# Attention over memory slots with a spatial gate: one load over all partitions each for k, v and phi, row reductions by halving, and a new written order

## The chip, the cores and the metric

The kernel runs on one core of a Trainium2 chip. The metric is the device time of one execution in microseconds (us). The engines are named as the profile names them: PE (TensorE, matmuls), PEld (its weight loads), DVE (VectorE), ACT (ScalarE), POOL (GpSimd) and SP (SyncE), whose queue SPq issues every transfer of this kernel.

## What is computed

The inputs are q, k, v of 8 batches x 8 heads x 576 rows x 64, and phi of 8 x 8 x 576 x 32. Cut to what matters:

```python
a = softmax(phi, over the 576 rows)                 # the maximum and the sum run over rows
k_m, v_m = a^T k, a^T v                             # 32 x 64 for each head
attn = softmax(q k_m^T / 8, over the 32 slots)
x = attn v_m, heads side by side                    # 8 x 576 x 512
h = relu(x w_in);  u, v = the halves of h           # 512 columns each
v_n = (v - mean) / sqrt(var + 1e-6)                 # over columns
v_s = w_spatial v_n + b_spatial                     # over the 576 rows
out = (u * v_s) w_out
```

The weights w_in (512 x 1024), w_spatial (576 x 576) and w_out (512 x 512) are the same for all batches. w_in and w_out arrive as 64-bit numbers, which the kernel turns into 32-bit ones by shifts, masks and multiplications ("decode").

## The kernel before

The work is cut into small generator functions, one step to each `yield`, named by a letter: P `memory_weights` (load of phi, its softmax), K `memories` (loads of k and v, k_m and v_m), Q `queries`, S `scores`, M `products` (v_m times w_in, so that x w_in becomes attn times that), V `gate`, U `units`, G `spatial`, O `project`. For the weights: D `load_win`, L and E decode of the two column halves of w_in, X load and decode of w_out, W and T w_spatial and its transposes, B the bias.

The order on every engine is written out by hand. START is the order of the prologue, of the whole of batch 0 and of what batch 1 needs meanwhile. PLAN is played once for each further batch; a prime marks the next batch, two primes the one after. All engines work off their instructions in this order, SP its transfers too. The set ON_VECTOR says which steps go to DVE; those not in it go to POOL, ACT or PE.

Products that need more than one pass of precision are split in a high and a low part, and the low part (`ml`, `wtl`, `ws`, `al`, `vl`, `gl`) is a difference. On DVE it is one subtraction. Elsewhere PE subtracts the high part in PSUM by a matmul with a negative identity (`minus`) and ACT copies the rest.

Names in the rows: `raw` is w_in as it arrives, `power` and `win_sb` are its decode, `raw_out` is w_out; `phi_sb` and `kv_sb` hold phi, k and v of one batch; `mx` is the maximum over the 9 row groups of a partition, `mt`, `cm`, `cmb` and `mb` finish it over partitions; `es` is the sum of the exponentials; `kvm` is the product of phi with k and v (72 matmuls a batch, then 8 with `ones` for the sum); `sc` are the scores, `sm` the scores turned, `aT`, `ah`, `al` the attention; `mp` is products' PSUM, `mh` and `ml` its parts; `pu`, `pv`, `ps`, `po` are the PSUM tiles of units, gate, spatial and project. `mp0` and `mp1` below are the two column halves of mp. There are four single-bank PSUM buffers (`bank`), which sc, mp, mt, mb, kvm, tk, tv, pv and po take in turn, and two double ones for wt, pu and ps.

A transfer of phi, k or v of a batch is two: heads of even number to partitions 0 to 63, heads of odd number to partitions 64 to 127. The queries of batch 0 come in a layout of their own: whole rows of 64 numbers, read once for either half of the columns, in 12 transfers; those of the other batches come in 4 transfers, in pieces of 32 numbers.

Of the kernel before, what the change touches and what calls it, by code (L numbers as in the profile page):

```python
# [51 lines left out]
    E0.add E1.add L0.add L0.mul ml001 wtl0 X0.add X1.add X1.mul X2.wol X3.mul ml110 ml111 ml100  # L52
    ml101
# [4 lines left out]
def memory_attention_spatial_gate(  # L58
# [12 lines left out]

# [349 lines left out]
    def queries(b, _):  # L421
        qT = None
        if b == 0:

            tiles = [
                one.tile([P, n, NX * D + 32], F32, tag=tag, name="q_all")
                for n, tag in ((4, "q_sb"), (2, "mh"), (2, "ml"))
            ]
            h = 0
            for x in tiles:  # L430
                n = x.shape[1]
                for c in range(2):
                    for g in range(2):
                        rows = slice(64 * c + 32 * g, 64 * c + 32 * g + 32)
# [4 lines left out]
                    yield  # L439
                h += n  # L440
            parts = [
                x[:, 2 * n : 2 * n + 2, 32:].rearrange("p h (i d) -> p h i d", d=D)[:, :, :, 0:32]
                for x in tiles
                for n in range(x.shape[1] // 2)
            ]
        else:
            q_sb = one.tile([P, H, NX, 32], F32, name="q_sb")
            for c in range(2):
                for g in range(2):
                    rows = slice(64 * c + 32 * g, 64 * c + 32 * g + 32)  # L450
                    nc.sync.dma_start(
                        q_sb[rows].rearrange("p h i d -> p (h i) d"),
                        q[b, :, :, 32 * g : 32 * g + 32].rearrange(
# [337 lines left out]
```

## Time and profile before

| | us |
|---|---|
| median of 3 runs | 441.12 (441.07 to 441.49) |
| the profiled execution | 442.75 |
| its span, first to last instruction | 440.9 |
| PE busy | 403.1 (91%) |
| DVE busy | 302.3 (69%) |
| ACT busy | 222.9 (51%) |
| POOL busy | 70.3 (16%) |

The span is that of the instructions; the execution's time has 1.8 us more around it. PE is the engine with most work, but its idle time is not spread over the span: the busy shares in 40 slices show it idle in the first five to six slices of 11 us and full from there on.

### The profile page before, as it was taken

How to read it: one execution, taken by the hardware profiler on the slowest of the kernel's cores; microseconds unless marked ns; L12 is line 12 of the kernel's file. 1: busy time of each engine (PE TensorE's matmuls, PEld its weight loads, DVE VectorE, ACT ScalarE, POOL GpSimd, SP SyncE). 2: the span in 40 equal slices, each digit the busy share in tenths (PEclk: the TensorE clock that was granted, in tenths of full speed). 3: DMA queues.
4: the chain of work that ended last, by engine and by line, in shares of the span. 5: the costliest groups of instructions: out<-in, count | busy, mean ns of one | idle time of the engine just before them, and what ended most of it. 6: DMA issues, size and time to landing. Idle time of an engine off the chain costs nothing.

```text
span 440.9 us, 9251 instructions
## 1 busy us (share of the span) xinstructions
PE 403.1 (91%) x3815; PEld 336.2 (76%) x3815; DVE 302.3 (69%) x501; ACT 222.9 (51%) x427; POOL 70.3 (16%) x147
## 2 busy tenths in 40 slices
PE   1425699999999999999999999999999999999996
PEld 1313178788879888898889887988798887988984
DVE  0973998998599538994699439955897457824420
ACT  3552367764583429532764248343843367336412
POOL 2033214430210004000400022001400021003000
PEclk9999999999999999999999999999999999999999
DMA  8999999922999129912992159903990300010003
GB/s 252 361 210 219 210 188 185 232 22 76 177 167 111 48 77 196 165 15 97 178 170 31 73 133 169 125 24 114 175 163 16 104 3 1 1 71 26 1 3 118
DMA packets 86863, 51.88 MB, mean 118 GB/s; under 512 B 66786, under 2 KB 70882, under 8 KB 86820
## 3 DMA queue, kind: packets, MB, share of 16 engines
q1 hardware_dynamic: 86820, 51.28, 58.5%
q8 instruction: 30, 0.49, 0.5%
q14 instruction: 13, 0.11, 0.1%
HBM read 41.83 MB, written 9.44 MB: 116 GB/s over the span
## 4 chain that ended last, share of the span: by engine, by line
PE 83%; DMA 11%; DVE 2%; ACT 2%; SPq 1%; issue 1%; POOL 0%; DVEq 0%; ACTq 0%; POOLq 0%
PE ps L658 27%; PE po L698 22%; PE pv L571 12%; PE pu L620 11%; PE kvm L365 4%; DMA q_all<-in_q_dram 4%; DMA kv_sb<-in_v_dram 3%; PE mp L541 3%; DMA raw<-in_moe_w_in_dram 2%; PE sc L480 2%; DMA phi_sb<-in_phi_dram 1%; DVE mx L322 1%; SPq L352 0%; DVE vl L598 0%; ACT vr L593 0%
## 5 line engine op out<-in xcount | busy, mean ns | idle before, releaser
L658 PE MATMUL ps<-wth,vh 128*128 128x288 f32 x256 | 57.8, 307 | 0.1
L658 PE MATMUL ps<-wtl,vh 128*128 128x288 f32 x256 | 54.9, 296 | 0.0
L658 PE MATMUL ps<-wth,vl 128*128 128x288 f32 x256 | 54.6, 295 | 0.0
L583 POOL TENSOR_SCALAR rs<-mv 128x1 f32<-128x1 f32 (+1 forms) x40 | 8.8, 221 | 269.4 <-DVE mv L580 245.2
L698 PE MATMUL po<-woh,gh 128*128 128x512 f32 x128 | 49.9, 390 | 0.0
L698 PE MATMUL po<-woh,gl 128*128 128x512 f32 x128 | 49.9, 390 | 0.0
L698 PE MATMUL po<-wol,gh 128*128 128x512 f32 x128 | 49.8, 389 | 0.0
L704 ACT COPY o<-po 128x512 f32<-128x512 f32 x36 | 21.1, 589 | 54.7 <-PE po L698 53.9
L658 PEld LDWEIGHTS ps<-wth,vh 128*128 128x128 f32 x256 | 40.6, 189 | 10.0 <-issue 5.0
L578 DVE BATCH_NORM_STATS2 st<-vr 128x6 f32<-128x512 f32 (+1 forms) x40 | 27.3, 681 | 27.5 <-ACT vr L575 27.5
L680 ACT CAST gh<-g 128x512 fp32r<-128x512 f32 x32 | 19.1, 620 | 50.9 <-DVE g L669 50.9
L658 PEld LDWEIGHTS ps<-wtl,vh 128*128 128x128 f32 x256 | 41.3, 189 | 0.0
L658 PEld LDWEIGHTS ps<-wth,vl 128*128 128x128 f32 x256 | 41.3, 188 | 0.0
L629 ACT ACTIVATE u<-pu 128x576 f32<-128x576 f32 x32 | 20.2, 658 | 30.8 <-PE pu L620 30.4
L593 ACT ACTIVATE vr<-vr,sh,rs 128x512 f32<-128x512 f32 (+1 forms) x40 | 31.8, 816 | 4.8 <-POOL sh L588 4.8
L365 PE MATMUL kvm<-kv_sb,phi_sb 64*32 64x128 f32 x1152 | 24.9, 309 | 8.8 <-DMA kv_sb<-in_v_dram 8.8
L571 PE MATMUL pv<-mh,ah 128*128 128x512 f32 (+1 forms) x80 | 31.8, 397 | 0.0
L571 PE MATMUL pv<-mh,al 128*128 128x512 f32 (+1 forms) x80 | 31.6, 395 | 0.0
L571 PE MATMUL pv<-ml,ah 128*128 128x512 f32 (+1 forms) x80 | 31.6, 395 | 0.0
L365 PEld LDWEIGHTS kvm<-kv_sb,phi_sb 64*32 64x32 f32 x1152 | 19.5, 118 | 15.4 <-DMA kv_sb<-in_v_dram 9.3
L669 DVE TENSOR_TENSOR g<-u,ps 128x576 f32<-128x576 f32 x32 | 24.0, 752 | 10.1 <-PE ps L658 9.8
L682 DVE TENSOR_TENSOR grl<-g,grh 128x64 fp32r<-128x64 f32 x32 | 6.7, 212 | 34.8 <-ACT grh L680 34.8
(130 smaller groups left out, 896.3 us busy)
## 6 DMA issues: line engine op xcount, KB each, us to landing
kv_sb<-in_k_dram SPq DMA_DIRECT2D x16, 576.0 KB, 8.7
kv_sb<-in_v_dram SPq DMA_DIRECT2D x16, 576.0 KB, 8.3
out_dram<-o SPq DMA_DIRECT2D x32, 256.0 KB, 2.0
q_sb<-in_q_dram SPq DMA_DIRECT2D x28, 288.0 KB, 8.2
phi_sb<-in_phi_dram SPq DMA_DIRECT2D x16, 288.0 KB, 4.9
raw<-in_moe_w_in_dram SPq DMA_DIRECT2D x8, 512.0 KB, 7.5
raw_out<-in_moe_w_out_dram SPq DMA_DIRECT2D x4, 512.0 KB, 9.9
w_sb<-in_moe_w_spatial_dram SPq DMA_DIRECT2D x1, 1152.0 KB, 5.7
```

The source lines that it names most:

```text
L365: nc.tensor.matmul(kvm[r][32 * j : 32 * j + 32], phi_sb[halves[r], j, i, :], kv_sb[halves[r], j, :, i * D : (i + 1) * D], start=(i == 0), ...
L541: nc.tensor.matmul(mps[r][32 * j : 32 * j + 32, :], vT[D * r : D * r + D, 32 * j : 32 * j + 32], win_sb[D * r : D * r + D, j, cs], start=True,
L571: nc.tensor.matmul(pv, x[:, r, cs], m[:, r, DM:DFF], start=(n == 0), stop=(n == 5))
L578: nc.vector.bn_stats(st6, vr)
L593: nc.scalar.activation(vr, vr, AF.Identity, bias=sh, scale=rs)
L620: nc.tensor.matmul(pu[:, hf, 0:HALF], m[:, r, cs], a[:, r, hf * HALF : (hf + 1) * HALF], start=(n == 0), stop=(n == 5),)
L629: nc.scalar.activation(u[:, dt, :].rearrange("p (a s) -> p a s", a=2), pu[:, :, 0:HALF], AF.Relu)
L658: nc.tensor.matmul(ps[:, hf, 0:HALF], a, w[:, hf * HALF : (hf + 1) * HALF], start=(n == 0), stop=(n == len(ops) - 1),)
L669: nc.vector.tensor_tensor(g.rearrange("p (a s) -> p a s", a=2), u[:, dt, :].rearrange("p (a s) -> p a s", a=2), ps[:, :, 0:HALF], op=ALU.mult,
L680: nc.scalar.copy(hi, x)
L698: nc.tensor.matmul(po, a, w, start=(n == 0), stop=(n == 11))
L704: nc.scalar.copy(o, po)
```

## The change

Four edits, and a new order:

- phi, k and v of a batch come in one transfer each over 128 partitions (two heads side by side) in place of two over 64.
- q of batch 0 is loaded as in the other batches: 4 transfers in pieces of 32 numbers, 1.18 MB in all, in place of 12 transfers that move 2.36 MB.
- The maximum and the sum over a partition's 9 row groups are four elementwise instructions (`over_rows`: 4 groups against 4, 2 against 2, 1 against 1, and the ninth) in place of one reduction. `es` takes `mx`'s buffer. The sum of batch 1 runs on POOL, the others on DVE.
- START is written anew; PLAN differs only in that three P steps stand where one stood ahead (`P'*4`, `P''*4`). In ON_VECTOR the last multiplication of E's decode moves from POOL to DVE, and three low parts change places (`ml001` to `ml000`, `wtl0` to `wtl2`, `X2.wol` to `X3.wol`).

```diff
-        for r in range(2):
-            nc.sync.dma_start(
-                phi_sb[64 * r : 64 * r + 64].rearrange("p j i m -> p j (i m)"),
-                phi[b].rearrange("(j r) (p i) m -> r p j (i m)", r=2, i=NX)[r],
-            )
+        nc.sync.dma_start(
+            phi_sb.rearrange("p j i m -> p j (i m)"),
+            phi[b].rearrange("(j r) (p i) m -> (r p) j (i m)", r=2, i=NX),
+        )
...
-        nc.vector.tensor_reduce(mx, phi_sb.rearrange("p j i m -> p j m i"), axis=AX.X, op=ALU.max)
-        yield
+        yield from over_rows(nc.vector, mx, ALU.max)
...
-        es = state["es", b] = one.tile([P, NJ, MEM], F32, name="es")
-        nc.vector.tensor_reduce(es, phi_sb.rearrange("p j i m -> p j m i"), axis=AX.X, op=ALU.add)
-        yield
+        es = state["es", b] = one.tile([P, NJ, MEM], F32, tag="mx", name="es")
+        yield from over_rows(engine(f"es{b}"), es, ALU.add)
...
+    def over_rows(eng, to, op):
+        half = one.tile([P, NJ, 4, MEM], F32, name="half")
+        eng.tensor_tensor(half, phi_sb[:, :, 0:4], phi_sb[:, :, 4:8], op=op)
+        yield
+        eng.tensor_tensor(half[:, :, 0:2], half[:, :, 0:2], half[:, :, 2:4], op=op)
+        yield
+        eng.tensor_tensor(to, half[:, :, 0], half[:, :, 1], op=op)
+        yield
+        eng.tensor_tensor(to, to, phi_sb[:, :, 8], op=op)
+        yield
...
-            for r in range(2):
-                nc.sync.dma_start(
-                    kv_sb[64 * r : 64 * r + 64, :, n, :],
-                    x[b].rearrange("(j r) (p i) d -> r p j (i d)", r=2, i=NX)[r],
-                )
+            nc.sync.dma_start(
+                kv_sb[:, :, n, :], x[b].rearrange("(j r) (p i) d -> (r p) j (i d)", r=2, i=NX)
+            )
...
-        if b == 0:
...
-                        nc.sync.dma_start(
-                            x[rows, :, 32 - 32 * g : 32 - 32 * g + NX * D],
-                            q[b, h : h + n].rearrange("h (c x i) d -> c x h (i d)", c=2, i=NX)[c],
-                        )
...
+        q_sb = one.tile([P, H, NX, 32], F32, name="q_sb")
+        for c in range(2):
+            for g in range(2):
...
+                    q[b, :, :, 32 * g : 32 * g + 32].rearrange(
+                        "h (i c x) d -> c x (h i) d", c=2, x=32
+                    )[c],
...
-    P' K' U0 V1 V0 K' U0 V2 U0 K' U2 V0 V1 U1 V1 V0 V2 V1 V2 K' V0 V4 U1 V1 V3 Q' K' V0 P'' V1
+    P'*4 K' U0 V1 V0 K' U0 V2 U0 K' U2 V0 V1 U1 V1 V0 V2 V1 V2 K' V0 V4 U1 V1 V3 Q' K' V0 P'' V1
```

The first transfers of SP, before: w_spatial first, then phi, all of w_in, k, v, q of batch 0, and then phi, k and v of batch 1.

```order
1 L257 DMA w_sb<-in_moe_w_spatial_dram 128x4x576
2 L258 DMA w_rem<-in_moe_w_spatial_dram 64x576
3 L260 DMA b_sb<-in_moe_b_spatial_dram 1x576 x2
4 L316 DMA phi_sb<-in_phi_dram 64x4x288 x2
5 L175 DMA raw<-in_moe_w_in_dram 128x1024 x8
6 L352 DMA kv_sb<-in_k_dram 64x4x576 x2
7 L352 DMA kv_sb<-in_v_dram 64x4x576 x2
8 L435 DMA q_all<-in_q_dram 32x4x576 x4
9 L435 DMA q_all<-in_q_dram 32x2x576 x8
10 L316 DMA phi_sb<-in_phi_dram 64x4x288 x2
11 L352 DMA kv_sb<-in_k_dram 64x4x576 x2
12 L352 DMA kv_sb<-in_v_dram 64x4x576 x2
```

The same stretch of SP now:

```order
1 L174 DMA raw<-in_moe_w_in_dram 128x1024
2 L326 DMA phi_sb<-in_phi_dram 128x4x288
3 L256 DMA w_sb<-in_moe_w_spatial_dram 128x4x576
6 L174 DMA raw<-in_moe_w_in_dram 128x1024 x4
7 L359 DMA kv_sb<-in_k_dram 128x4x576
8 L174 DMA raw<-in_moe_w_in_dram 128x1024
9 L359 DMA kv_sb<-in_v_dram 128x4x576
10 L174 DMA raw<-in_moe_w_in_dram 128x1024 x2
11 L432 DMA q_sb<-in_q_dram 32x72x32 x4
12 L326 DMA phi_sb<-in_phi_dram 128x4x288
13 L359 DMA kv_sb<-in_k_dram 128x4x576
14 L359 DMA kv_sb<-in_v_dram 128x4x576
```

k and v of batch 0 moved ahead of the last three parts of w_in, phi ahead of w_spatial; the order of q, phi, k and v behind them is kept.

DVE, before, between the scores of batch 0 and the first product of units:

```order
33 L491 STREAM_TRANSPOSE sm<-sc_0_0_352 128x288
37 L322 TENSOR_REDUCE mx<-phi_sb 128x128
38 L497 TENSOR_REDUCE rmx<-sm 128x36
41 L336 TENSOR_TENSOR phi_sb<-phi_sb,mb_393 128x1152
45 L510 TENSOR_TENSOR sm<-sm,rsum 128x1152
46 L519 STREAM_TRANSPOSE aT<-sm 128x9x32 x2
47 L346 TENSOR_REDUCE es<-phi_sb 128x128
48 L523 TENSOR_TENSOR al<-aT,ah 128x576
53 L523 TENSOR_TENSOR al<-aT,ah 128x576
```

The same stretch now:

```order
36 L315 TENSOR_TENSOR half<-phi_sb 128x512
39 L466 STREAM_TRANSPOSE sm<-sc_0_0_344 128x288
43 L321 TENSOR_TENSOR mx<-mx,phi_sb 128x128
44 L472 TENSOR_REDUCE rmx<-sm 128x36
47 L345 TENSOR_TENSOR phi_sb<-phi_sb,mb_397 128x1152
51 L162 TENSOR_TENSOR ws_96<-wt_308,ws_95 64x512
52 L485 TENSOR_TENSOR sm<-sm,rsum 128x1152
53 L493 STREAM_TRANSPOSE aT<-sm 128x9x32 x2
54 L162 TENSOR_TENSOR ml<-mp_0_0_423,mh 128x512
57 L499 TENSOR_TENSOR al<-aT,ah 128x576
61 L499 TENSOR_TENSOR al<-aT,ah 128x576
```

Three of the four steps of mx stand ahead of the transposes of the scores, es is gone from DVE (it is on POOL for batch 1), and one ws and one ml stand in the stretch.

ACT in the same place now; the buffer that the second half of mp1 (`mp_1_1`) holds is free when its ml is copied:

```order
38 L477 ACTIVATE sm<-sm 128x1152
39 L526 CAST mh<-mp_1_1_375 128x512
40 L352 ACTIVATE phi_sb<-phi_sb 128x1152
41 L294 CAST ws_95<-wt_308 128x512
42 L294 CAST ws_95<-wt_308 128x64
43 L160 CAST wtl<-wt_338 128x512
44 L294 CAST wth<-wt_338 128x64
45 L160 CAST ml<-mp_1_1_375 128x512
46 L526 CAST mh<-mp_0_0_423 128x512
```

Before, both halves of mp followed phi's exponential there and stood ahead of the k and v products on PE; now mp1 stands ahead of it and mp0 behind it, and mp0 is followed on PE by the 72 kvm of batch 1, their 8 with ones, one subtraction of mp0's high part, and the first units.

## Rows read from the trace of the kernel before

**Rows 1.** Engines by stretch; last columns: clock share, busy share of DMA engines, GB/s.

```profile
3.00:5.40 2.40, 0.00 (x0) 0.00 (x0) 0.00 (x0) 0.00 (x0) 0.00 (x0) 1.00 1.04 412
6.20:8.60 2.40, 1.38 (x5) 0.90 (x5) 0.00 (x0) 1.20 (x3) 0.47 (x1) 1.00 1.11 217
12.00:16.00 4.00, 3.19 (x12) 2.22 (x12) 3.43 (x7) 2.62 (x5) 0.00 (x0) 1.00 1.03 410
22.00:36.00 14.00, 5.37 (x161) 4.33 (x161) 8.55 (x10) 5.67 (x8) 5.81 (x4) 1.00 1.05 210
62.00:66.00 4.00, 4.00 (x65) 3.79 (x50) 3.59 (x10) 2.62 (x7) 1.20 (x1) 1.00 1.09 120
0.00:62.80 62.80, 29.89 (x422) 17.26 (x422) 41.80 (x56) 28.52 (x51) 14.06 (x20) 1.00 1.03 246
62.80:440.90 378.10, 373.25 (x3410) 318.92 (x3393) 260.54 (x446) 194.38 (x377) 56.20 (x127) 1.00 0.52 96
```

**Rows 2.** Chain that ended last, 15 to 90 us: start, duration, what.

```profile
20.31 16.87 DMA q_all<-in_q_dram
...
42.24 15.36 DMA kv_sb<-in_v_dram
```

**Rows 3.** Timeline of PE: start, duration, count, idle before and its releaser.

```profile
44.31 2.13 PE L480 MATMUL sc<-qT,kT 64*32 64x288 f32 x20 [1.87 <-DVE qT L469]
...
51.61 3.70 PE L541 MATMUL mp<-win_sb,vT 64*32 64x512 f32 x32
...
57.83 2.38 PE L365 MATMUL kvm<-kv_sb,phi_sb 64*32 64x128 f32 x78 [0.43 <-DMA kv_sb<-in_v_dram]
...
62.82 0.85 PE L620 MATMUL pu<-ah,mh 128*128 128x288 f32 x2
...
81.74 1.45 PE L541 MATMUL mp<-win_sb,vT 64*32 64x512 f32 x16 [0.54 <-DVE sm L491]
...
108.15 1.37 PE L365 MATMUL kvm<-kv_sb,phi_sb 64*32 64x128 f32 x80
```

**Rows 4.** Transfers: queue, count, size, median us from issue to landing.

```profile
w_sb<-in_moe_w_spatial_dram SPq DMA_DIRECT2D x1, 1152.0 KB, 5.7
```

**Rows 5.** Timeline of DVE in the prologue.

```profile
24.12 0.68 DVE L184 TENSOR_SCALAR power<-raw 128x1024 int32<-128x1024 int32 x1
24.73 1.21 DVE L215 SCALAR_TENSOR_TENSOR win_sb<-win_sb,raw 128x1024 f32<-128x1024 f32 x1
25.86 0.68 DVE L190 TENSOR_SCALAR win_sb<-raw 128x1024 int32<-128x1024 int32 x1
...
45.51 1.81 DVE L491 STREAM_TRANSPOSE sm<-sc 128x288 f32<-128x288 f32 x4
...
51.95 1.35 DVE L336 TENSOR_TENSOR phi_sb<-phi_sb,mb 128x1152 f32<-128x1152 f32 x1
...
62.42 0.76 DVE L523 TENSOR_TENSOR al<-aT,ah 128x576 fp32r<-128x576 f32 x1
```

**Rows 6.** Groups of DVE by form: count, busy us, mean ns of one, idle before.

```profile
L682 DVE TENSOR_TENSOR gl<-g,gh 128x512 fp32r<-128x512 f32 x32 | 20.8, 683 | 0.9 <-ACT gh L680 0.7
...
L322 DVE TENSOR_REDUCE mx<-phi_sb 128x128 f32<-128x1152 f32 x8 | 17.9, 2240 | 10.2 <-DMA phi_sb<-in_phi_dram 9.9 <-issue 0.3
L346 DVE TENSOR_REDUCE es<-phi_sb 128x128 f32<-128x1152 f32 x8 | 17.7, 2213 | 0.0
...
L682 DVE TENSOR_TENSOR grl<-g,grh 128x64 fp32r<-128x64 f32 x32 | 6.7, 212 | 34.8 <-ACT grh L680 34.8
```

**Rows 7.** Timeline of ACT and of POOL in the prologue.

```profile
53.33 1.17 ACT L343 ACTIVATE phi_sb<-phi_sb 128x1152 f32<-128x1152 f32 x1
...
56.07 0.59 ACT L161 CAST ml<-mp 128x512 fp32r<-128x512 f32 x1
...
45.50 2.49 POOL L223 TENSOR_TENSOR win_sb<-win_sb,power 128x512 f32<-128x512 f32 x2 [2.23 <-DVE wtl L163]
```

More of the change, by code (lines that the diff above doesn't have):

```diff
@@ new lines @@
+    L0*2 E1 W P D0 L0 T2 P W D0 T1*2 E0 K T2 T1 E0 P W Q E1*2 L0 T1 E1 P L0 P E1 T1 E0*2 K T1 L1
+    E0 Q K E1 P' L1 K L0 T2 L1 T1 E1 L1*2 K W E1 T4 K*2 L1 Q*3 K Q K'*2 P' K*2 P' T0 S P' S T0
+    S*3 P' M1 P' S M1 T0 M1 P'*2 L1 P' M1 S P' S B M1 S L1 S P' T4*2 X1 T4*2 X0 T0 S M1 T0 M0 P'
+    M1 P' S M0 K' T0 T4 M0 S M0 T0 T4 P' S M0 S*3 X0*2 S X0 P' S K' M0 X1 U0 X1*2 X0 U1 V1 M0 X0
+    Q' V0 X1 X0 V1 X0 K'*2 V1 K' V0 X1*2 K' Q' U0 U1 X0 V3 U1 K' X1 U0 K' V1*2 U2 V2 V0 X1 V3*2
+    V4 V1*2 X0 K'*2 V0 Q'*2 V0*3 V4 U3 U2 V2 Q' U3 X1 X0 Q' U2 V4 V3*2 U3 S' V2 S'*2 X1 S' V2 S'
@@ L39 @@
+    P'' X2 V2 X2 S' Q'' G0 X3 G1 M0' V3 V4 M1' V3 V2 V4*2 V2 P'' M1' X2 V4*2 K'' M0' G1 X2*2 M0'
+    G0 P'' M1' G1 M1' P'' G0 P'' G1 G0 P'' M0' K'' G1 G3 X3 G0 S' G2 X2 P'' G1 G0 G3 X2 M1' G1
+    X2 G0 M0' G2 M1' X3 G1 P'' G3 M0' P'' G2 G3 G0*2 G1 P'' G2 X2 M0' S' X3 G3 X3*2 X2 X3 O3 G2
+    S' X3 O2 G2 G3 M1' G2 O1 X2 O0 X3*2 G3*2 G2 X3 G2 O3 S' P'' S' O1 S'*2 O3*2 P'' S' O1 O2 S'
+    O0 S'*2 P'' O2 S'*2 P'' O1 G3 O2 P'' O0*2
 """
 PLAN = """
-    P' K' U0 V1 V0 K' U0 V2 U0 K' U2 V0 V1 U1 V1 V0 V2 V1 V2 K' V0 V4 U1 V1 V3 Q' K' V0 P'' V1
@@ L48 @@
+    U1 K' U3 U2 V1 Q' V4 V2 V3 K' V2 V4 V3 K'*2 P''*4 U3 V4 K' S' U2 U3 V2 V3 V4 K'' S' V3 S'*2
+    G0 V4 V3 G1 P'' S' M0'*2 Q'' P'' M1' G0 S' V2 S' M1' V4 G1 M1' V4 G0 V3 S' G1 Q G0 M1' M0'
+    M1' P'' S' G1 G0 P'' M1' G2 S' G1 K'' G1 M0' S' G0 S' G1 G0*2 Q'' G3 G0 G2 S' G1 G3 G1 G2 G3
+    G2 P'' S' G2*2 M1' G3*2 O3 G3 S'*2 O0 S' G2 G3 O1 O0 G3 P'' S' O0 S' O0 O1 O3 G3 Q'' O3 O4
+    M0' G2 O3 O2 O1 V0' G2 O4 M0'*2 O1 O4 V0' Q'' O2 O4 O2*2
 """
@@ L51 @@
     """
[L52 to L53 removed]
+    es0 E0.add E0.mul E1.add E1.mul L0.add L0.mul ml000 wtl2 X0.add X1.add X1.mul X3.wol ml110
+    ml111 ml100 ml101 es2 es3 es4 es5 es6 es7
     """.split()
@@ L421, in queries @@
     def queries(b, _):
-        qT = None
-        if b == 0:
[L425 to L434, printed above, removed]
-                        nc.sync.dma_start(
-                            x[rows, :, 32 - 32 * g : 32 - 32 * g + NX * D],
-                            q[b, h : h + n].rearrange("h (c x i) d -> c x h (i d)", c=2, i=NX)[c],
-                        )
[L439 to L453, printed above, removed]
-                            "h (i c x) d -> c x (h i) d", c=2, x=32
-                        )[c],
-                    )
-                yield
-            parts = [
-                q_sb[:, 2 * n : 2 * n + 2].rearrange("p h i d -> p (h i d)") for n in range(4)
-            ]
@@ L461, in queries @@
-        for n in range(4):
-            if qT is None:
-                qT = state["qT", b] = one.tile([P, H, HALF], F32, name="qT")
-            to = qT[:, 2 * n : 2 * n + 2]
-            if b == 0:
-                to = to.rearrange("p h (i x) -> p h i x", x=32)
-            else:
-                to = to.rearrange("p h s -> p (h s)")
-            nc.vector.transpose(to, parts[n])
+        q_sb = one.tile([P, H, NX, 32], F32, name="q_sb")
+        for c in range(2):
+            for g in range(2):
+                rows = slice(64 * c + 32 * g, 64 * c + 32 * g + 32)
+                nc.sync.dma_start(
+                    q_sb[rows].rearrange("p h i d -> p (h i) d"),
+                    q[b, :, :, 32 * g : 32 * g + 32].rearrange(
+                        "h (i c x) d -> c x (h i) d", c=2, x=32
+                    )[c],
+                )
+            yield
@@ L470, in queries @@
+        qT = state["qT", b] = one.tile([P, H, HALF], F32, name="qT")
+        for n in range(4):
+            nc.vector.transpose(
+                qT[:, 2 * n : 2 * n + 2].rearrange("p h s -> p (h s)"),
+                q_sb[:, 2 * n : 2 * n + 2].rearrange("p h i d -> p (h i d)"),
+            )
             yield
```

23 lines of the change are left out of this document (4 added, 19 removed).

## The prediction

> **What bounds the kernel now.** I read the engines by stretch first. Up to 62.8 us PE is busy 29.89 us, from there to the end 373.25 of 378.10 us [rows 1]. So the second part is PE's own work, which the change leaves alone (same matmuls, and after batch 0 the same order of them), and there is nothing to win there but the last 4.9 us; what can move is the 62.8 us ahead. There the DMA engines are full (share 1.03) and yet move only 246 GB/s [rows 1]. The same rows say why: the transfer of w_spatial runs at 412 GB/s and w_in at 410, but the stretch in which k, v and q of batch 0 arrive runs at 210 [rows 1]. The chain of waits agrees: of its time before the steady part, 16.87 us is q of batch 0 and 15.36 us v of batch 1 [rows 2]. PE's timeline shows the end of it: kvm of batch 1 waits for v until 57.83, and right behind it, at 62.82, the first units start and PE stays full [rows 3]. DVE is not far from being the bound as well: the last `al`, which those units read, ends at 62.42 + 0.76 = 63.2 [rows 5].
>
> **Transfers.** w_spatial's is a 128 x 4 x 576 transfer, and so is k's now, with the same 2,304-byte pieces; I therefore take w_spatial's rate, 412, rounded to 400, for k, v and phi. Bounds: 210 as now (217 for phi) and 412 [rows 1]. k and v, 1.18 MB each, then take 3.0 us each for 5.6, phi (0.59 MB) 1.5 for 2.7. q of batch 0 gets pieces of 128 bytes; batch 1's q, loaded like that, moves at 120 GB/s [rows 1], so 1.18 MB take 9.8 us, against 2.36 MB at 210 = 11.2 us now. [...]
>
> Now the queue in its new order, from the first issue. w_spatial was issued at 0.72 us and landed 5.7 us later [rows 4], of which 3.0 are its bytes; so a landing is 3.4 us plus the bytes ahead at their rates. w_in in eighths is 1.3 us each. Sums: w_in 1.3, phi 2.8, w_spatial 6.1, four eighths 11.3, k 14.3, an eighth 15.6, v 18.5, two eighths 21.1, q 30.9, phi of batch 1 32.4, k 35.4, v 38.4. Landed: the sixth eighth at 19.0, v at 21.9, all of w_in at 24.5, q at 34.3, v of batch 1 at 41.8 in place of 57.6. The transfers stop being the bound for that last one, and DVE and ACT are next.
>
> **DVE up to the queries.** The sixth eighth completes the second half of E's bits, and its shift is where DVE waits last. From 19.0 DVE then has, up to the transposes of q: 4 shifts or masks of 1,024 at 0.61, 7 two-operation instructions at 1.13 (starts of neighbours [rows 5]), 3 multiplications of the same size (E's two are new here, POOL had them; 2.49 us for half as much there [rows 7]) at 1.13, the sum by halving, and small ones of 0.6 together. Halving costs 512, 256, 128 and 128 numbers: 0.6 for 512 (0.68 less overlap) and 0.2 for 64 [rows 6] give 0.6 + 0.33 + 0.2 + 0.2 = 1.3, against 2.2 for one reduction; strided reads could at worst make that equal, 2.2. Sum 2.4 + 7.9 + 3.4 + 1.3 + 0.6 = 15.6, so 34.6, just behind q's landing at 34.3. Four transposes of q at 0.7: 37.4. The scores start then and 1.3 us later `sm` can begin (44.31 less 0.13 to 45.51 before [rows 3, 5]); three steps of `mx` fit in between: 38.7.
>
> **DVE from the scores to the units.** Before, from the start of `sm` to the end of the last `al`: 45.51 to 63.18, 17.7 us. Out of it go `mx` (2.0; 0.2 stays) and `es` (2.1, now on POOL); in come a `ws` and an `ml`, 0.6 each, and 0.15 of small ones. 17.7 - 4.1 + 0.2 + 1.35 = 15.2, so the last `al` ends at 53.9. `es` on POOL is two to three times 1.25 (2.49 for two instructions of 512 [rows 7]), some 3 us beside DVE, done long before the units.
>
> **ACT and PE in the same place.** phi of batch 1 less its maximum ended 51.95 + 1.35 - 45.51 = 7.8 us after `sm` began [rows 5]; without `mx` that is 6.0, so 44.7. Then ACT: the exponential 1.17 [rows 7], and ahead of the copy of `ml` that frees the buffer of the second half of mp1 two large copies and two small, with the copy 1.8 us (0.5 each from 0.59 with overlap, [rows 7]): 47.7. PE then runs mp0, half of 3.70 [rows 3], to 49.6, and the kvm of batch 1 with what follows: from 57.83 to 62.82 it took 5.0 [rows 3], with two more ahead 5.1. Units start at 54.7, after POOL's `es` and about with DVE's `al`, which only their second halves read. So the order on PE and ACT ends last, by under 1 us: 62.8 - 54.7 = 8.1 us gained. Had PE the pace that it has later (40 kvm in 1.37, 8 mp in 0.95 [rows 3]), this path would be 3 us shorter and DVE the bound: at best 2 us more gain. At worst the hand-overs that I left out cost 0.1 to 0.2 each, some 2 us.
>
> **From there to the end.** Before, PE waited 0.54 us for `sm` at 81.74 [rows 3]; in the new order `sm` stands ahead of `mx`, and that wait should go. The third and fourth parts of w_out stand in SP behind q of batch 1 and wait for the split of the first two, about 11 and 15 us after the units start; project needs them over 35 us after, so this is hidden; if not, project waits, 1 to 3 us. In batches 1 to 7 DVE saves about 1 us twice a batch, beside full PE: nothing. The new waits of `mx`'s third step (for the ones product of the batch before, since `es` shares the buffer) and of phi's transfer (as before) block nothing on DVE but steps that wait for phi anyway.
>
> **Sum.** 8.1 + 0.5 = 8.6 us less in the profiled execution: 440.9 to 432.3 in its span, 442.75 to 434.2 in its time. The median of the runs, 441.12, lies 1.6 us under that execution; I take the difference off the median and give back 0.3 us for hand-overs: **432.8**.
>
> **Rivals.**
> 1. One transfer of 128 partitions is no faster than two of 64. [...] For it: phi's two halves, at 217, moved no better than k's [rows 1]. Against it: w_spatial's 412. Then k and v take 5.6 and phi 2.7: the sixth eighth lands 3.8 us later, q 6.4 later, at 40.7, where DVE comes to it at 38.4, and v of batch 1 at 54.6, an us ahead of its use. All behind q is 6.1 us later than forecast: units at 60.8, a gain of 2.0 + 0.5, and with the 0.3 given back 438.9.
> 2. The long tail: the units start as forecast, but something behind them waits (w_out's parts, the last `vl`), since DVE is as full there as before: 1 to 3 us, 434 to 437.
> 3. Slower: q of batch 0 in small pieces lands late. It stands ahead of phi, k and v of batch 1 in one queue, and DVE's transposes of q, and all behind them on DVE, wait. q lands 0.3 us before DVE comes to it, so each us more is a us lost. To use up the 8.6 us and 0.9 more it needs 9.8 + 9.8 us, a rate of 60 GB/s: half of what rows 1 show. It decides there; the time would be 442.5.
>
> **How the numbers follow.** Chances: the forecast (430 to 434.5) 0.68, rival 2 0.15, rival 1 0.08, rival 3 with other ways to be slower 0.06, and 0.03 that two of these meet near no change. The range 429.5 to 437.0 takes in the forecast, its best case of 2 us more and rival 2. About 0.2%, 0.9 us, is what a measurement of this kernel can tell from no change: faster by more 0.91, within it 0.03, slower by more 0.06.
>
> **What would show it.** After: over 350 GB/s while k and v arrive, q of batch 0 in about 10 us, no wait of PE for v, a wait of PE ahead of mp0 for ACT, the first units at 54 to 56 us, and PE full from there, with as many us to the end as now, 378. Wrong would be: k and v at 210; units after 58 us; PE's busy time after them under its 98.7%.

## The result and the profile after

| us | before | after |
|---|---|---|
| median | 441.19 (441.07 to 441.49) | 435.11 (434.80 to 435.84) |
| the profiled execution | 442.75 | 435.84 |
| its span | 440.94 | 434.06 |
| first units on PE | 62.82 | 57.77 |
| from there to the end | 378.1 | 376.3 |
| DVE busy | 302.3 | 294.9 |
| POOL busy | 70.3 | 74.0 |

The change makes the kernel faster: the ratio of after to before is 0.9864 (95% interval 0.9845 to 0.9884), about 6 us. The median after is that of three executions; a fourth, at 1348 us, stands far outside and no comparison uses it (with it in, the median reads 435.48). The forecast was 432.8 with a range of 429.5 to 437.0.

The page of after, part 2, the busy tenths in 40 slices of 10.9 us and the granted clock of TensorE:

```profile
PE   0436699999999999999999999999999999999996
...
PEclk9985689999999999999999999999999999999999
```

PE is full from the sixth slice on, as before; what was gained is half a slice ahead of it. The third to sixth slices have a granted clock at or between the two levels (2.4 GHz is the 9 or more, 1.2 GHz the 5); before, all 40 slices read 9. The engines by stretch, with the columns of [rows 1] (last three: granted clock, busy share of the DMA engines, GB/s):

```profile
16.00:22.00 6.00, 1.62 (x6) 1.11 (x6) 4.45 (x9) 4.75 (x9) 0.00 (x0) 1.00 1.04 405
24.00:32.00 8.00, 3.65 (x153) 2.74 (x136) 7.97 (x13) 3.84 (x7) 0.00 (x0) 0.87 1.09 140
36.00:41.00 5.00, 4.09 (x33) 2.08 (x35) 4.97 (x7) 1.13 (x3) 4.84 (x4) 0.50 1.05 392
57.80:434.10 376.30, 372.43 (x3394) 316.38 (x3392) 251.76 (x480) 194.86 (x378) 59.91 (x128) 1.00 0.41 95
```

From 16 to 22 us, where by the order of the queue k, the sixth part of w_in and v of batch 0 arrive, the transfers keep 405 GB/s; from 36 to 41 us, with k and v of batch 1 and no w_in among them, 392. Before, k, v and the old q moved at 210 [rows 1]. From 24 to 32 us q of batch 0 arrives in its small pieces at 140. Three of PE's waits before the units (what waits <- for what: us in total, times, longest):

```profile
PE kvm L371 <- DMA kv_sb<-in_v_dram: 5.0, 1, 5.0
PE mp L157 <- ACT mh L526: 2.2, 1, 2.2
...
PE mp L517 <- DVE sm L466: 1.5, 1, 1.5
```

The wait for v is that of batch 0, at 18.4 to 23.4 us. The wait for v of batch 1, which ended at 57.83 before [rows 3], is gone. What ends last now is told by the chain of waits (start, duration, what):

```profile
10.96 9.32 DMA raw<-in_moe_w_in_dram
20.37 0.70 DVE power L183
...
35.18 2.32 DVE power L206
...
43.43 0.40 DVE sm L466
...
52.97 0.50 ACT ml L160
53.51 3.67 PE kvm L371 x129
```

From 20.37 us, when the sixth eighth of w_in has landed, to 43.4 us DVE alone is the chain, without a hole of more than 0.3 us; then PE and ACT take turns until the units. [rows 2] had two transfers of 15 and 17 us in that place.

### The profile page after: what moved, and what is told of

Its sections match the earlier page's. It is cut to its first block, busy times and chain, and to the rows that moved or that the text cites. A ratio compares the mean times of both kernels' runs of the same rounds, so it can differ in the third digit from the quotient of the medians.

```text
span 434.1 us, 9211 instructions
## 1 busy us (share of the span) xinstructions
PE 400.4 (92%) x3815; PEld 333.1 (77%) x3815; DVE 294.9 (68%) x546; ACT 223.0 (51%) x427; POOL 74.0 (17%) x148
## 4 chain that ended last, share of the span: by engine, by line
PE 87%; DVE 6%; DMA 4%; ACT 1%; issue 1%; SPq 0%; DVEq 0%; ACTq 0%
PE ps L634 28%; PE po L674 23%; PE pv L547 13%; PE pu L596 12%; PE kvm L371 4%; PE mp L517 4%; DMA raw<-in_moe_w_in_dram 2%; DMA w_rem<-in_moe_w_spatial_dram 2%; PE sc L455 2%; DVE power L206 1%; DVE win_sb L214 1%; DVE win_sb L219 1%; DVE qT L441 1%; DVE half L317 0%; DVE g L645 0%
## 5 line engine op out<-in xcount | busy, mean ns | idle before, releaser
L634 PE MATMUL ps<-wth,vh 128*128 128x288 f32 x256 | 57.8, 307 | 0.1
L559 POOL TENSOR_SCALAR rs<-mv 128x1 f32<-128x1 f32 (+1 forms) x40 | 10.1, 253 | 262.7 <-DVE mv L556 238.0
L674 PE MATMUL po<-wol,gh 128*128 128x512 f32 x128 | 50.8, 397 | 0.0
L634 PEld LDWEIGHTS ps<-wth,vh 128*128 128x128 f32 x256 | 40.4, 188 | 10.9 <-issue 5.9
L596 PE MATMUL pu<-ah,mh 128*128 128x288 f32 x128 | 29.2, 309 | 0.0
L371 PE MATMUL kvm<-kv_sb,phi_sb 64*32 64x128 f32 x1152 | 23.3, 300 | 5.8 <-DMA kv_sb<-in_v_dram 5.0
```

Of the source, the lines that this page charges most:

```text
L371: nc.tensor.matmul(kvm[r][32 * j : 32 * j + 32], phi_sb[halves[r], j, i, :], kv_sb[halves[r], j, :, i * D : (i + 1) * D], start=(i == 0), ...
L596: nc.tensor.matmul(pu[:, hf, 0:HALF], m[:, r, cs], a[:, r, hf * HALF : (hf + 1) * HALF], start=(n == 0), stop=(n == 5),)
L634: nc.tensor.matmul(ps[:, hf, 0:HALF], a, w[:, hf * HALF : (hf + 1) * HALF], start=(n == 0), stop=(n == len(ops) - 1),)
L674: nc.tensor.matmul(po, a, w, start=(n == 0), stop=(n == 11))
```

## Experiments

Times are medians of four executions (three for after, six for kernel 9, ten for kernel 1); the ratio is to the kernel before in the same series, with its 95% interval. The last four columns are of the profiled execution, the first of them its time.

| kernel | us | ratio | profiled | `sm` of batch 0 starts | first units | units to end |
|---|---|---|---|---|---|---|
| before | 441.2 to 441.5 | 1 | 442.75 | 45.51 | 62.82 | 378.1 |
| after | 435.11 | 0.9864 (0.9845 to 0.9884) | 435.84 | 43.35 | 57.77 | 376.3 |
| 1: after, two loads of 64 partitions | 441.82 | 1.0009 (0.9995 to 1.0023) | 442.74 | 49.55 | 63.36 | 377.6 |
| 2: before, one load of 128 partitions | 434.59 | 0.9842 (0.9828 to 0.9857) | 434.47 | 39.57 | 54.27 | 378.4 |
| 3: after, two loads over 128 partitions | 435.42 | 0.9863 (0.9849 to 0.9878) | 435.61 | 43.48 | 57.07 | 376.8 |
| 4: after, L1's steps on DVE | 435.11 | 0.9847 (0.9831 to 0.9864) | 436.08 | 40.30 | 57.52 | 376.8 |
| 5: after, maximum as one reduction | 434.43 | 0.9831 (0.9808 to 0.9853) | 434.47 | 42.31 | 55.56 | 377.1 |
| 6: kernel 2, q of batch 0 in pieces | 433.48 | 0.9813 (0.9792 to 0.9834) | 433.53 | 40.29 | 54.69 | 377.1 |
| 7: kernel 6, both reductions by halving | 436.12 | 0.9863 (0.9833 to 0.9893) | 436.14 | 40.45 | 58.27 | 376.1 |
| 8: after, w_spatial later | 435.01 | 0.9855 (0.9824 to 0.9885) | 434.03 | 41.50 | 56.24 | 376.0 |
| 9: 5 and 8 together | 434.61 | 0.9842 (0.9817 to 0.9867) | 435.87 | 42.25 | 56.97 | 377.1 |

One kernel's executions lie up to 3.2 us apart (kernel 9: 433.12 to 436.29), and the profiled one of after and of kernels 1, 4 and 9 lies 0.7 to 1.3 us above its median, that of kernel 8 1.0 below. So the starts of `sm` and of the units tell what one execution did; whether a kernel is faster is told by the ratios. The intervals of kernels 2, 3, 4, 5, 7, 8 and 9 all overlap that of after.

### Which edit carries the gain: kernels 1, 2 and 3

Kernel 1 is the changed kernel with the loads of phi, k and v cut again into two of 64 partitions:

```diff
...
-            nc.sync.dma_start(
-                kv_sb[:, :, n, :], x[b].rearrange("(j r) (p i) d -> (r p) j (i d)", r=2, i=NX)
-            )
+            for r in range(2):
+                nc.sync.dma_start(
+                    kv_sb[64 * r : 64 * r + 64, :, n, :],
+                    x[b].rearrange("(j r) (p i) d -> r p j (i d)", r=2, i=NX)[r],
+                )
```

> The changed kernel with phi, k and v again in two transfers of 64 partitions each; all else as changed. Theory (a transfer over 128 partitions moves twice as fast, and that is what frees the prologue): the stretch of k and v falls back from about 400 to about 210 GB/s, the last part of E's bits lands near 24 us in place of 20.3, q 6 us later, and the first units start 4 to 6 us later than 57.8; 439 to 441 us. Rival (the new written order carries the gain, the loads are hidden): first units within 1 us of 57.8, 435 to 436 us.

Kernel 2 is the other way round: the kernel before with that edit alone, old order, old q, reductions as they were.

> The kernel before with nothing changed but phi, k and v in one transfer over 128 partitions each. Theory (transfer rate): k and v take 3 us each in place of 5.6, phi 1.5 in place of 2.7, so q of batch 0 lands some 6 us earlier (about 37 in place of 43.4) and v of batch 1 some 13 us earlier; then DVE's chain to the last al is the bound, and the units start at 57 to 58 in place of 62.8: 435 to 437 us. Rival (the order is what counts): units at 61 to 63, 439 to 441 us.

Kernel 3 is the changed kernel with k and v in two transfers each, cut by heads, so that either covers all 128 partitions:

```diff
-            nc.sync.dma_start(
-                kv_sb[:, :, n, :], x[b].rearrange("(j r) (p i) d -> (r p) j (i d)", r=2, i=NX)
-            )
+            for g in range(2):
+                nc.sync.dma_start(
+                    kv_sb[:, 2 * g : 2 * g + 2, n, :],
+                    x[b].rearrange("(j r) (p i) d -> (r p) j (i d)", r=2, i=NX)[
+                        :, 2 * g : 2 * g + 2
+                    ],
+                )
```

> The changed kernel with k and v in two transfers each again, but cut by heads, so that each goes over all 128 partitions (half the bytes each). Theory (it is the number of partitions that sets the rate): about 400 GB/s while k and v arrive, and the time of the changed kernel, 435 to 436 us. Rival (it is the number and size of transfers): 210 to 300 GB/s there and 437 to 440 us.

Measured: without the wide loads nothing of the gain is left (1.0009), with them alone all of it is there (0.9842 against 0.9864, with intervals that overlap). Kernel 1 came out just above the 439 to 441 us expected, with the units 5.6 us later; kernel 2 came out below its 435 to 437, with the units 3 us earlier than expected; kernel 3 as expected. The stretch from 17 to 21 us of kernel 1, where k of batch 0 arrives, in the columns of [rows 1], has the old rate back; the stretch from 16 to 22 us of kernel 3, as in after, does not:

```profile
17.00:21.00 4.00, 1.62 (x6) 1.10 (x6) 2.43 (x3) 3.18 (x5) 0.00 (x0) 1.00 1.06 211
```

```profile
16.00:22.00 6.00, 1.62 (x6) 1.11 (x6) 4.45 (x9) 4.61 (x9) 0.00 (x0) 1.00 1.05 408
```

So it is the partitions under one transfer that set the rate, not the number of transfers: 64 partitions move at 211 GB/s, 128 at 392 to 408, with one transfer or with two. The first rival is out. Fewer than 64 did not lower the rate further: before, the old q came over 32 partitions at a time, and in a stretch with nothing else under way it moved at 211, too:

```profile
32.00:37.00 5.00, 3.74 (x158) 3.65 (x138) 0.00 (x0) 0.00 (x0) 2.77 (x3) 1.00 1.05 211
```

The Trainium skill, "SBUF — State Buffer", section "Door 1: The DMA port swizzle", says that the rate depends on how many of 16 ports the partitions reach and that bit 6 of the partition's number picks one half of these ports or the other. By it a load of partitions 0 to 63 has half of the ports, and the trace agrees: 211 is 0.52 of 405.

With these three kernels the other edits are weighed as a whole, too: on top of kernel 2 they move the units from 54.27 to 57.77, 3.5 us later, and give 2.1 us back behind them. PE's last wait ahead of the units ends at 51.27 in kernel 2 and at 53.51 in after, so 2.24 of the 3.5 us lie ahead of it. The other 1.26 are PE's pace: the same 159 or 160 matmuls from there to the units, in kernel 2, in after and in before (PE's busy time first, granted clock third from the end):

```profile
51.27:54.27 3.00, 3.00 (x160) 2.35 (x160) 3.00 (x4) 2.12 (x4) 0.00 (x0) 1.00 1.26 153
```

```profile
53.51:57.77 4.26, 4.26 (x159) 4.20 (x160) 4.16 (x11) 2.73 (x5) 1.48 (x3) 0.57 0.02 4
```

```profile
57.83:62.82 4.99, 4.99 (x160) 4.15 (x160) 4.96 (x9) 2.94 (x6) 0.00 (x0) 1.00 1.30 189
```

Before, they take 4.99 us at a granted clock that reads 1.00, so 1.99 of the 8.55 us by which kernel 2's units come earlier than before's are PE's pace and not the transfers' time. The next runs look for the 2.24 us.

### DVE and POOL get in each other's way: kernels 4 and 5

DVE's timeline in after (start, duration, line, operation, shapes, count):

```profile
35.18 2.32 DVE L206 SCALAR_TENSOR_TENSOR power<-raw,power 128x1024 int32<-128x1024 int32 x1
37.43 2.75 DVE L441 STREAM_TRANSPOSE qT<-q_sb 128x576 f32<-128x576 f32 x4
40.10 0.65 DVE L315 TENSOR_TENSOR half<-phi_sb 128x512 f32<-128x512 f32 x1
40.78 1.38 DVE L317 TENSOR_TENSOR half<-half 128x256 f32<-128x256 f32 x1
42.19 1.23 DVE L319 TENSOR_TENSOR mx<-half 128x128 f32<-128x128 f32 x1
```

Instructions of the same kinds and sizes some 15 us earlier, where POOL is idle:

```profile
21.70 0.42 DVE L317 TENSOR_TENSOR half<-half 128x256 f32<-128x256 f32 x1
...
22.64 1.22 DVE L206 SCALAR_TENSOR_TENSOR power<-raw,power 128x1024 int32<-128x1024 int32 x1
23.78 0.28 DVE L319 TENSOR_TENSOR es<-half 128x128 f32<-128x128 f32 x1
```

2.32 against 1.22, 1.38 against 0.42, 1.23 against 0.28: 3.0 us more for three instructions. POOL's timeline has the last steps of L1, the second half of a column half of w_in, just there:

```profile
34.80 3.84 POOL L212 TENSOR_TENSOR win_sb<-win_sb,raw 128x512 f32<-128x512 f32 x2 [32.35 <-ACT raw L204]
...
40.21 3.07 POOL L222 TENSOR_TENSOR win_sb<-win_sb,power 128x512 f32<-128x512 f32 x2
```

Before, two of them took 2.49 [rows 7]. Kernel 4 puts these two steps on DVE:

```diff
-    es0 E0.add E0.mul E1.add E1.mul L0.add L0.mul ml000 wtl2 X0.add X1.add X1.mul X3.wol ml110
+    es0 L1.add L1.mul E0.add E0.mul E1.add E1.mul L0.add L0.mul ml000 wtl2 X0.add X1.add X1.mul X3.wol ml110
```

> The changed kernel with the addition and the last multiplication of L1's decode moved from POOL to DVE (about 2.3 us more work on DVE before the scores, one conversion less on ACT, POOL empty there). Theory (DVE instructions that ran beside POOL's were slowed: 2.32, 1.38 and 1.23 us where 1.2, 0.4 and 0.3 are usual, 3 us in all): these three return to their usual time and DVE's turn of the scores begins 0 to 1 us earlier than 43.35; 434 to 435.5 us. Rival (they were slow for another reason): they stay slow, the turn begins 2 us later, 437 to 438 us.

DVE's timeline of kernel 4:

```profile
35.14 1.22 DVE L206 SCALAR_TENSOR_TENSOR power<-raw,power 128x1024 int32<-128x1024 int32 x1
...
39.63 0.42 DVE L317 TENSOR_TENSOR half<-half 128x256 f32<-128x256 f32 x1
40.09 0.29 DVE L319 TENSOR_TENSOR mx<-half 128x128 f32<-128x128 f32 x1
40.30 1.57 DVE L466 STREAM_TRANSPOSE sm<-sc 128x288 f32<-128x288 f32 x4
...
43.42 1.22 DVE L214 SCALAR_TENSOR_TENSOR win_sb<-win_sb,raw 128x1024 f32<-128x1024 f32 x1
```

With POOL idle all three are back at their usual length and `sm` starts 3.05 us earlier (0 to 1 us was expected, with L1's two instructions ahead of the scores). That is shown. The units gain only 0.25 of it, for L1's two instructions of 1.22 now stand on DVE behind `sm`, ahead of the `ws` that ACT waits for, and ACT's row says so:

```profile
51.77 0.21 ACT L294 CAST ws<-wt 128x64 fp32r<-128x64 f32 x1 [2.65 <-DVE ws L162]
```

In after that wait is 0.75, and the copy of `ml` behind it starts at 52.84, in kernel 4 at 52.46: nearly the same, from another cause. L1's two instructions are not all of it. `rsum`'s TENSOR_SCALAR, also ahead of `ws`, takes 1.25 us where it takes 0.18 in after, and it ends with POOL's first step of `es`; an earlier one, of the decode, takes 1.17 in place of 0.69, also beside POOL. DVE's and POOL's timelines of kernel 4:

```profile
13.56 1.17 DVE L183 TENSOR_SCALAR power<-raw 128x1024 int32<-128x1024 int32 x1 [6.12 <-DMA raw<-in_moe_w_in_dram]
...
49.53 1.25 DVE L482 TENSOR_SCALAR rsum<-rsum 128x36 f32<-128x36 f32 x1
```

```profile
12.77 1.40 POOL L306 TENSOR_TENSOR ws<-b_sb,ws 1x576 fp32r<-1x576 f32 x1 [10.32 <-ACT ws L304]
...
48.77 1.97 POOL L315 TENSOR_TENSOR half<-phi_sb 128x512 f32<-128x512 f32 x1 [34.59 <-ACT phi_sb L352]
```

Kernel 5 leaves POOL its steps and makes the maximum one reduction again (the three steps that fall away stay as empty places in the order):

```diff
-        yield from over_rows(nc.vector, mx, ALU.max)
+        nc.vector.tensor_reduce(mx, phi_sb.rearrange("p j i m -> p j m i"), axis=AX.X, op=ALU.max)
+        yield
+        yield
+        yield
+        yield
```

> The changed kernel with the maximum as one reduction again, in the place of the first of its four steps; the sum stays by halving. Theory (one reduction reads one operand and is not slowed beside POOL, the halving steps are): the reduction takes 2.1 us where the steps took 3.3 with their slow ones, the turn of the scores begins at 42.2 to 42.4 in place of 43.35, the units about 1 us earlier than 57.8: 434 to 435 us. Rival (halving is the faster way everywhere): 0.7 us or more later, 436 us.

DVE's and POOL's timelines of kernel 5 in the same place:

```profile
40.26 2.13 DVE L332 TENSOR_REDUCE mx<-phi_sb 128x128 f32<-128x1152 f32 x1
```

```profile
40.37 2.50 POOL L222 TENSOR_TENSOR win_sb<-win_sb,power 128x512 f32<-128x512 f32 x2
```

The reduction takes 2.13 us right beside POOL's multiplications, 2.24 on average over the eight of before [rows 6], and POOL's two keep their 2.5. The halving, four short instructions that look like 1.7 us in the trace of a quiet stretch, takes 3.5 in this place. `sm` starts 1.04 us earlier, as expected. The units come 2.2 us earlier, about 1 us was expected; 0.73 of the 2.2 are PE's pace (3.53 us from its last wait on, against 4.26). The kernel is at 434.43, but its interval and that of after overlap, so a gain in time is not shown by these two alone.

The three instructions that were slowed in after have two tensors as inputs (`raw` and `power`, two parts of `half`), and the two kinds that were not, the reduction and the transposes, have one. The Trainium skill, "SBUF — State Buffer", section "SBUF: two separate sides", has this as a rule: DVE and GpSimd share one pair of ports, which a DVE instruction with two SBUF inputs, or in a 2-port mode, and a GpSimd instruction hold in turn, each for its whole length. The rows agree: 1.10, 0.96 and 0.94 us more for the three, each somewhat less than one POOL instruction of 1.25. Two inputs are not the whole condition, for the two TENSOR_SCALARs that waited in kernel 4 have one; whether they ran in such a mode no row here tells. The rule was at hand before the prediction, and the prediction did not use it.

### q in pieces, and halving in the old order: kernels 6 and 7

Kernel 6 is kernel 2 with the q of batch 0 in 4 transfers of small pieces, at the places of the order before:

```diff
-        if b == 0:
...
-            for x in tiles:
...
-                        nc.sync.dma_start(
-                            x[rows, :, 32 - 32 * g : 32 - 32 * g + NX * D],
-                            q[b, h : h + n].rearrange("h (c x i) d -> c x h (i d)", c=2, i=NX)[c],
-                        )
...
+        q_sb = one.tile([P, H, NX, 32], F32, name="q_sb")
...
+                    q[b, :, :, 32 * g : 32 * g + 32].rearrange(
+                        "h (i c x) d -> c x (h i) d", c=2, x=32
+                    )[c],
...
```

> The kernel before with one transfer over 128 partitions each for phi, k and v, and with q of batch 0 in pieces of 32 numbers as in the changed kernel; its transposes stand in the old places of the old order. Theory (rate): in the run with the wide loads alone the last transpose of q starts at 37.5 us, after 2.8 us of waiting; 1.18 MB at some 135 GB/s land about 3 us earlier than 2.36 MB at 210, all at once, so that the last transpose ends near 35, and the first units start 2 to 3 us earlier than the 54.3 there: 431 to 433 us. Rival (small pieces cost as much as reading twice): units within 0.5 us of 54.3, 434 to 435 us.

DVE's timeline of kernel 2, then of kernel 6, where the last transposes of q stand (the first of the four in kernel 6, too):

```profile
37.54 0.78 DVE L466 STREAM_TRANSPOSE qT<-q_all 128x576 f32<-128x576 f32 x1 [2.83 <-DMA q_all<-in_q_dram]
```

```profile
35.03 0.78 DVE L435 STREAM_TRANSPOSE qT<-q_sb 128x576 f32<-128x576 f32 x1 [5.73 <-DMA q_sb<-in_q_dram]
...
37.11 1.42 DVE L435 STREAM_TRANSPOSE qT<-q_sb 128x576 f32<-128x576 f32 x2
```

The old q comes in parts, of which the last is late (37.5 us); the new one comes whole at 35.0, and DVE then has the four transposes together. Their ends differ by 0.2 us, and the units by 0.4. Half the bytes of q are worth nothing before the units, where 2 to 3 us had been expected. All the same the kernel is 1.1 us faster than kernel 2 (measured in another series, and the two intervals touch), behind the units (377.1 against 378.4 to the end); part of it is the first units' wait for a `wtl` of DVE, 0.40 us against 0.74. Kernel 6 is the fastest of the study, ahead of both kernels of the comparison: its interval, 0.9792 to 0.9834, lies clear of that of after.

Kernel 7 adds to kernel 6 the halving of both reductions, all on DVE, each as one step of the old order:

```diff
...
-        nc.vector.tensor_reduce(mx, phi_sb.rearrange("p j i m -> p j m i"), axis=AX.X, op=ALU.max)
+        over_rows(nc.vector, mx, ALU.max)
...
-        nc.vector.tensor_reduce(es, phi_sb.rearrange("p j i m -> p j m i"), axis=AX.X, op=ALU.add)
+        over_rows(nc.vector, es, ALU.add)
```

> All edits of the change but its new order: the kernel before with wide loads, q in pieces and both reductions by halving (all on DVE, four instructions in the place of the one), in the old order and with the old division among engines. Theory (halving saves 0.8 us an instruction where POOL is idle and loses 2 where POOL works on two operands beside it): the sum gains 0.8 us ahead of the units; the maximum stands beside POOL's last multiplication of w_in if q lands early, and then loses what it gains; 430 to 432.5 us in all, within 1.5 us of the kernel without halving. Then the new order would be what costs the changed kernel 3 us or more. Rival (the new order is needed with these edits): 434 to 437 us.

DVE's timeline of kernel 7, with POOL's L223 beside it (42.16, 3.18 us for two):

```profile
42.16 0.65 DVE L315 TENSOR_TENSOR half<-phi_sb 128x512 f32<-128x512 f32 x1
42.84 1.37 DVE L316 TENSOR_TENSOR half<-half 128x256 f32<-128x256 f32 x1
44.25 1.24 DVE L317 TENSOR_TENSOR mx<-half 128x128 f32<-128x128 f32 x1
```

The same lengthening as in after, in an order that is otherwise kernel 6's: 3.6 us for the maximum (42.16 to 45.73) in place of 2.0. It costs 2.6 us in all (436.12 against 433.48), and the units stand 3.6 us later. Of these 1.5 are DVE's; the rest is PE's pace. The stretch from the first kvm of batch 1 that waits no more to the units, in kernel 6 and in kernel 7 (PE's busy time first, granted clock third from the end):

```profile
51.62:54.69 3.07, 3.07 (x159) 2.35 (x159) 3.07 (x4) 2.13 (x4) 0.00 (x0) 1.00 0.45 42
```

```profile
53.27:58.27 5.00, 4.89 (x162) 3.59 (x161) 4.53 (x12) 3.24 (x7) 0.00 (x0) 0.60 0.07 8
```

The same 159 to 162 matmuls take 3.07 us at a granted clock of 1.00 (2.4 GHz) and 5.00 at 0.60, where most of the stretch lies on the lower level (0.50, 1.2 GHz). PE had waited 3.11 us for the maximum in kernel 6, 4.66 in kernel 7. That the longer wait is the cause is an inference: no run changes it alone.

Kernel 7 was expected at 430 to 432.5 us and missed it. It has all edits of the change but the new order and the new division among engines, and its time is that of after (0.9863 against 0.9864): these two are worth nothing that the runs can tell, and what the bundle loses against kernel 6, kernel 7 loses with halving alone.

### w_spatial later: kernels 8 and 9

In after the sixth eighth of w_in is ready at 20.37 us, behind phi, w_spatial and k. Kernel 8 moves W, T and B: the transfer of w_spatial behind w_in, k and v of batch 0, its transposes and splits behind the first product of batch 0. The head of START:

```diff
-    D1 P W T3 P T3 B D0 T3 D0 T3 P*2 D1 T3 T2 L0 P E0 D1 T2*2 P T2 T3*2 P K P E0*2 L0 D1 P*2 K
+    D1 P*2 D0*2 P*2 D1 L0 P E0 D1 P*2 K P E0*2 L0 D1 P*2 K L0*2 E1 P D0 L0 P D0 W E0 K E0 P
```

> The changed kernel with w_spatial's transfer moved behind w_in, k and v in SP's queue, and the steps that transpose and split it moved behind the first product of batch 0, in their own order. Theory (up to the scores DVE's chain starts with the landing of w_in's parts, and w_spatial's 1.3 MB ahead of them delay it by 3.3 us): the wait for E's last bits ends 3 us earlier (17 in place of 20.3), and the turn of the scores begins 2 to 3 us earlier; 432 to 433.5 us. Rival (ACT and PE, which now have the splits later, become late): 435 to 437 us.

DVE's timeline of kernel 8:

```profile
15.71 0.70 DVE L184 TENSOR_SCALAR power<-raw 128x1024 int32<-128x1024 int32 x1 [2.12 <-DMA raw<-in_moe_w_in_dram]
...
28.73 0.69 DVE L163 TENSOR_TENSOR wtl<-wt,wth 128x512 fp32r<-128x512 f32 x1 [1.92 <-ACT wth L295]
...
33.00 2.32 DVE L207 SCALAR_TENSOR_TENSOR power<-raw,power 128x1024 int32<-128x1024 int32 x1
...
38.17 1.68 DVE L316 TENSOR_TENSOR half<-phi_sb 128x512 f32<-128x512 f32 x1
```

The eighth is ready 4.66 us earlier, but `sm` starts only 1.85 earlier: 1.92 go into a new wait for `wth`, most of the rest into the splits (`wtl`) that now stand in this stretch, and POOL's steps still meet DVE's. The units stand at 56.24, but the time of 435.01 is that of after and not the 432 to 433.5 expected.

Kernel 9 has both edits, the one reduction of kernel 5 and the order of kernel 8, to see whether their gains of 2.2 and 1.5 us at the units add up.

> The changed kernel with two edits at once: the maximum is one reduction again, and the transfer of w_spatial stands behind w_in, k and v of batch 0, its transposes and bias steps behind the memories of batch 0. Each edit alone brought the first units 1.5 to 2.2 us forward (57.77 to 55.56 and 56.24). Theory A (DVE's chain up to `sm` sets the units, and both edits shorten it in different places): the gains add in part, units at 54 to 55 us, about 433 to 434 us in all. Theory B (behind `sm` the copy of `ml` on ACT is late anyway, as kvm of batch 1 waited 1.77 us for it with the second edit alone): no earlier than with the reduction alone, units at 55.5 us and 434.4 us. In both, the 376.3 us from the units to the end stay.

In this execution they don't: units at 56.97, later than with either alone. It took 435.87 us, 1.26 above the kernel's median of 434.61, which is no other than those of 5 and 8. `sm` starts at 42.25, as with kernel 5; of the shift of kernel 8, 0.96 us is missing from the start, for the same eighth of w_in, at the same place in the queue, was ready at 16.67 and not at 15.71. From `sm` on kernels 5 and 9 part. The stretch from the kvm that waited for ACT's `ml` to the units, in kernel 5 and in kernel 9:

```profile
52.03:55.56 3.53, 3.52 (x159) 3.48 (x160) 3.50 (x10) 1.98 (x4) 1.51 (x3) 0.70 0.46 44
```

```profile
52.40:56.97 4.57, 4.57 (x160) 4.51 (x160) 4.45 (x12) 2.90 (x5) 1.50 (x3) 0.51 0.22 23
```

The same matmuls, 3.53 us at 0.70 and 4.57 at 0.51. So 1.04 us of the 1.41 between their units are PE's pace, and 0.37 the copy of `ml`. The gains did not add, against the first theory. The second has the time (434.6 for 434.4) but not the reason: the units came 1.4 us later than it allowed for, and mostly by PE's pace, not by the copy of `ml`. How much of this is the kernel and how much the one execution is open.

## Why the prediction was right in the sign and 2.3 us too low

The sign and the mechanism were right: the transfers of phi, k and v stop being the bound, v of batch 1 is not waited for, DVE and the hand-overs behind it come next. That the time lies in the range is in part luck. 435.11 is above the 430 to 434.5 of the forecast itself, in the room that was left for rival 2, whose cause did not come up; the units, at 57.77, missed the 54 to 56 that were to show it and stayed 0.2 us short of the 58 that were to prove it wrong; and 5.8 us of errors on the late side met 2.7 on the early side. Nor did the forecast ask what each edit is worth alone: the wide loads by themselves give as much (kernel 2). The sizes, against the profiled execution's own time, as they were summed:

| step | forecast | measured |
|---|---|---|
| rate of k and v | 400 GB/s | 392 to 405 |
| q of batch 0 | 120 GB/s, 9.8 us | 140 GB/s, 8.4 us |
| DVE starts on the sixth eighth of w_in | 19.0 | 20.37 |
| from there to the transposes of q | 15.6 | 17.06 |
| from there to the start of `sm` | 4.1 | 5.92 |
| from there to phi less its maximum | 6.0 | 6.1 |
| from there to the end of the copy of `ml` | 3.0 | 4.0 |
| from there to the units | 7.0 | 4.3 |
| units | 54.7 | 57.77 |
| units to the end | 377.6 | 376.3 |

**Transfers.** Right in their rates; w_spatial's rate carried over to k, and q was a little better than its row. The eighth came 1.4 us late: the chain has 8.76 us from issue to landing for the last part of w_spatial and 9.32 from there for w_in, where the forecast took 3.4 us plus the bytes ahead; over 2 to 20 us the transfers moved 378 GB/s on average, not 400. DVE did not wait for q at all.

**DVE up to `sm`.** This is the step that failed. The two terms together came out 3.28 us too small, and 3.0 of these are the three instructions beside POOL (1.10 + 0.96 + 0.94). The forecast priced DVE's operations by rows in which POOL was idle or DVE had one input, and took halving as 0.6 + 0.33 + 0.2 + 0.2. It named POOL as the engine that E's multiplications were taken from and that `es` went to, and asked nothing of L1's, which stayed there. [rows 7] did not show the cost: beside POOL's two multiplications at 45.50 DVE, before, only turns the scores and reduces, operations with one input, which were not slowed.

**ACT and PE.** The copy of `ml` came 1.0 us later after phi than forecast; 0.75 of it is the wait of `ws` for DVE's `ws`, a hand-over that was left out. The place of the wait was wrong: mp0 did not wait for the copy but the kvm behind it did, as PE's row shows, and so the forecast's 1.85 us of mp0 lay beside the wait.

```profile
50.35 1.96 PE L517 MATMUL mp<-win_sb,vT 64*32 64x512 f32 x16
...
53.51 3.85 PE L371 MATMUL kvm<-kv_sb,phi_sb 64*32 64x128 f32 x135 [0.82 <-ACT ml L160]
...
57.77 0.42 PE L596 MATMUL pu<-ah,mh 128*128 128x288 f32 x2
```

Behind it kvm to the units took 4.3 us, against 5.1 forecast, at a granted clock of 0.57. Of the two errors 1.7 us on the early side are left. "The order on PE and ACT ends last, by under 1 us" did not quite hold: DVE's last `al` ended at 58.10, 0.33 us behind the start of the units, and nothing waited for it. The best case, PE at its later pace, was counted wrongly in the text ([rows 3] has 80 kvm in 1.37 us, not 40), but its size was sound: in kernels 2 and 6 PE had that pace there, 3.0 us in place of 5.0.

**From the units to the end.** 0.5 us was forecast, 1.8 came. The wait of 0.54 for `sm` [rows 3] is gone, as forecast: PE waits for nothing between 57.8 and 90.1 us. Another 0.6 is the start: the first three pairs of pu went from 62.82 to 64.23 before and from 57.77 to 58.56 after. Both lie ahead of project, which starts 32.3 us behind the units instead of 34.4; the other 0.9 us of that is in small pieces that no run told apart.

**The sum.** Units 3.07 us late, 1.3 given back behind them: the profiled execution is 435.84 where 434.2 was forecast. The remaining 0.6 us of the 2.3 is the step from the profiled execution to the median. Before's lay 1.63 us above its median, and the forecast took that off; after's lies 0.73 above its own, and 0.3 had been added for hand-overs. The other sums of the prediction come out, but for the 442.5 of rival 3, which by its own terms is 442.3.

**Rivals.** The first, half the partitions as fast as all, gave way to kernels 1 to 3; its price was right: kernel 1, which has it, has its units at 63.36, 5.6 us later than after, and the prediction had worked out 6.1. The second, work behind the units that comes late, did not come up. The third, q as the bound, was far off, with 140 GB/s against the 60 at which it decides. What did eat over a quarter of the gain that was forecast was none of the three.

## What to carry to other kernels

Look at the rate of a transfer beside the number of partitions that it covers: here 64 partitions at a time meant 210 GB/s and 128 meant 400, whatever the number of transfers, and that edit alone was the whole gain. When an operation is put in place of another on DVE, ask what POOL does at that moment and how many tensors the operation reads; a reduction of 2.1 us beside POOL was better than four instructions that add up to 1.7 without it. The busy time of a DVE instruction has such a wait in it, so set it beside the same instruction elsewhere in the trace. Try each edit of a bundle alone on the old kernel: two of the four (wide loads and small q pieces) gave 433.48 us, and the whole bundle 435.11.
